# Moving statistics, short products and turns inside the key/value stage of a fused attention and GLU kernel

## The chip, the cores and the metric

The kernel runs on one core of a Trainium2 chip. The metric is the device time of one execution in microseconds. Five engines work beside each other, each through its own queue in order: TensorE (PE in the profile; its weight loads are PEld), VectorE (DVE), ScalarE (ACT), GpSimd (POOL) and SyncE (SP), which here issues DMA transfers. Engines wait for each other by semaphores.

## What is computed

One transformer block in float32 over 2048 rows x of 576 numbers: a layer norm, a linear attention of 32 heads of 18 numbers, and a gated branch that multiplies it.

```python
x = A_x
xn = _layernorm(x, axis=-1)
s = _A_ref(xn, A_wqkv, A_wo)
g = _silu(_B_ref(xn, B_w_gate, B_w_up, B_w_down))
return x + s * g
```

with, in the attention,

```python
phi = lambda t: jnp.where(t > 0, t + 1, jnp.exp(t)) + 1e-6
pq, pk = phi(q), phi(k)
kv = jnp.einsum("bhsd,bhse->bhde", pk, v)
z = jnp.einsum("bhsd->bhd", pk)
num = jnp.einsum("bhqd,bhde->bhqe", pq, kv)
den = jnp.einsum("bhqd,bhd->bhq", pq, z)[..., None] + 1e-6
o = num / den
return (lambda x, *d: x.transpose(*d))(o, 0, 2, 1, 3).reshape(B, S, D) @ wo
```

The branch B (gate, up, down with 4608 columns) takes most of the time and is not touched by the change.

## The kernel before

**Tiles and stages.** The rows are cut into 16 tiles of 128 (P). Four tiles are a block of 512 columns of the transposed x (TB = 4 blocks, TT = 4 tiles in each). The first 215 us or so are the attention, in stages: tiles 0 to 7 (keys and values), q of blocks 0 and 1, tiles 8 to 15 (N0 = 8), q of blocks 2 and 3, and the output products s. Then comes branch B. Every engine's instructions keep the order in which the program writes them (`keep_in_program_order`, line 120), so the order of the source is the order of each queue.

**A tile** (`kv_tile`, line 492). `x_mm(t, c)` multiplies x of tile t by the three parts c of the key and value weights, 14 products in each. `turn(t + 1)` and `place(t + 1)` prepare the next tile: from tile 4 on, TensorE turns the mean and the scale of each row into rows over all partitions (the tile `ms`, line 214: one product from `mv`, one from `st`), and `normalize` (line 228) subtracts and multiplies on VectorE (`x`, `xf_B`) and cuts the result into a high and a low word (`xo_B`, ScalarE and VectorE). `k_post` makes phi of the keys in two steps, c = 0 and c = 1: VectorE writes `e_k` and `pk`, ScalarE takes the exponential of `e_k` behind the second step, GpSimd adds both to the finished `pk`. `v_post` copies v into `va` on ScalarE, also in two steps (c = 1 and c = 2), and GpSimd fills `va`'s first column. `pk` and `va` take buffers from four slots, two tiles' worth. The list `mid_` runs between `place` and the second step of `k_post`; the list `end` between the third product group and the last `v_post`.

**Pairs.** In each even tile, behind the first product group, `kv_pair` adds the sums of the two tiles before to the bank `kv_a` (`kv_mm`, line 396): per tile ten products, two halves of five groups. Four groups have 72 columns, the fifth has 36. The halves go to two halves of the array's columns.

**Statistics.** `x_next(n)` (line 1427) does for an even n the statistics of tiles n and n + 1: four `BATCH_NORM_STATS2` (`bn`) and two aggregates (`mv`) on VectorE, a logarithm and an exponential on ScalarE (`st`), and four more small VectorE steps. From tile 4 on nothing else is left in it, so for odd n it does nothing. x itself comes in pairs of tiles by `load_x`, issued on SP behind tile 8 for tiles 12 and 13, and behind tile 10 for tiles 14 and 15.

**Forms of x.** `difference` and `form` make sums and differences of blocks (T1 to T4) for branch B. `form("T4")` at the end of tile 9 is one ScalarE copy (`xo_T`), VectorE's low words, and a store.

**q stages.** `q_store` and `q_hold` compute q of one block and group gi by 14 products; for gi = 4 (the columns of the fifth group, made together with k and v and kept in `qt`) there are four turns (line 526) instead. `phi` follows on ScalarE, VectorE and GpSimd. `q_store` also writes the result to memory by SP. The dictionaries `behind` (line 1492) and `ahead` (line 1521) list what runs behind each q step (block, group).

Of the kernel before, what the change touches and what calls it, by code (L numbers as in the profile page):

```python
# [31 lines left out]
WIDTHS = [GW, GW, GW, GW, D - 4 * GW]  # L32
# [59 lines left out]
def block_kernel(ctx, tc, x, xe, xt, wq_d, wkv_d, wo, wgu_d, wd_d, out):  # L92
# [9 lines left out]
    def own_bank(name):  # L102
        return ps.tile([P, 512], F32, tag="own", bufs=2, name=name)
# [18 lines left out]
    def act(*args, **kw):  # L122
        pin(nc.scalar.activation(*args, **kw))  # L123

    def vec(op, *args, **kw):
        pin(getattr(nc.vector, op)(*args, **kw))  # L126
# [42 lines left out]
    def spread(n0, n):  # L169

        bn = sb.tile([P, TT, 12], F32, tag="bn", bufs=2, name=f"bn_{n0}")
        mv = sb.tile([P, 2 * TT, 2], F32, tag="mv", bufs=4, name=f"mv_{n0}")
        for t in range(n):
            xs = xstat[(n0 + t) // 2][:, (n0 + t) % 2]
            for j in range(2):
                src = xs[:, j, 0:HALF] if n0 < TT else xs[:, j * HALF : (j + 1) * HALF]
                vec("bn_stats", out=bn[:, t, 6 * j : 6 * j + 6], in_=src)
            vec("bn_aggr", out=mv[:, t, :], in_=bn[:, t, :])
        st = sb.tile([P, 6, TT], F32, tag="st", bufs=4, name=f"st_{n0}")
        act(st[:, 0, 0:n], mv[:, 0:n, 1], AF.Ln, bias=eps_t)  # L180
        act(st[:, 2, 0:n], st[:, 0, 0:n], AF.Exp, scale=-0.5)
        vec("tensor_scalar", st[:, 1, 0:n], mv[:, 0:n, 1], LN_EPS, None, op0=ALU.add)
        mom[n0] = n, mv, st

    def scales(n0):

        n, mv, st = mom.pop(n0)
        v, r, c = (st[:, i, 0:n] for i in range(1, 4))
        if n == 1:
            vec("tensor_scalar", c, r, r, -0.5, op0=ALU.mult, op1=ALU.mult)  # L190
            vec("tensor_scalar", c, c, v, 1.5, op0=ALU.mult, op1=ALU.add)
            vec("tensor_scalar", c, c, r, None, op0=ALU.mult)
        else:
            vec("scalar_tensor_tensor", c, r, -0.5, r, op0=ALU.mult, op1=ALU.mult)
            vec("tensor_mul", c, c, v)
            vec("scalar_tensor_tensor", c, c, 1.5, r, op0=ALU.add, op1=ALU.mult)
        for t in range(n):
            scale_of[n0 + t] = mv[:, t, 0:1], c[:, t : t + 1]

    def center(n):  # L200

        if n >= TT:
            return
        xs = xstat[n // 2][:, n % 2]
        m, r = scale_of.pop(n)
        vec("tensor_scalar", xs, xs, m, r, op0=ALU.subtract, op1=ALU.mult)
# [85 lines left out]
    def difference(s, i):  # L292
        f = xf[s]
        nm, a, b, o = SUMS[i]
        vec("tensor_sub", f[o], f[a], f[b])
        f[nm] = f[o]
# [82 lines left out]
    acc = []  # L379
# [13 lines left out]
        act(e, e, AF.Exp, scale=-1.0)  # L393
        pool("tensor_add", o, o, e)

    def kv_mm(t):
        if t == 0:
            acc.append(own_bank("kv_a"))
        pk, va = pks.pop(t), vas.pop(t)
        for gi, wdt in enumerate(WIDTHS):  # L400
            for half in range(2):
                o, cs = kv_out(gi, half)
                mm(
                    o, va[:, 2 * gi + half, 0 : o.shape[0]],
                    pk[:, gi * GW + cs.start : gi * GW + cs.stop],
                    start=(t == 0 and gi == 0), stop=(t == S // P - 1),
                    skip_group_check=True,
                )
# [6 lines left out]
    pkv, pks, vas, es, qt = {}, {}, {}, {}, {}  # L415
# [76 lines left out]
    def kv_tile(t, mid_=(), end=()):  # L492

        ahead = t % (2 * TT) != 2 * TT - 1
        x_mm(t, 0)
        if t % 2 == 0:
            kv_pair(t)
        if ahead:
            turn(t + 1)
        k_post(t, 0)  # L500
        x_mm(t, 1)
        if ahead:
            place(t + 1)
            save(t + 1)
        run(list(mid_))
        k_post(t, 1)
        v_post(t, 1)
        x_mm(t, 2)
        run(list(end))
        v_post(t, 2)  # L510

    def kv_pair(t):

        for i in (t - 2, t - 1):
            if i in vas:
                kv_mm(i)

    ph, ph_d = {}, {}

# [20 lines left out]
    def q_store(tb, gi):  # L540
        if tb not in ph_d:
            ph_d[tb] = dr.tile([P, NHG, TBN], F32, name=f"phd_{tb}")
        o = gl_tile([P, TBN], f"ph_{tb}_{gi}")
        q_mm(tb, gi, o)
        dma(out=ph_d[tb][:, gi, :], in_=o)

    def q_hold(tb, i, gi):
        if tb not in ph:
            ph[tb] = big(i, [P, NHG, TBN], F32, f"ph_{tb}")
        q_mm(tb, gi, ph[tb][:, gi, :])  # L550
# [87 lines left out]
    def kv_wo(gi):  # L638

        if gi == 4:  # L640
            at["kvh"] = big(4, [P, 4, D], F32R, "kvh")
            at["kvl"] = big(5, [P, 4, D], F32R, "kvl")

            at["kv4"] = big(6, [P, 4, D], F32R, "kv4")
            pool("memset", at["kv4"][Q4:P, 1, :].bitcast(F32), 0.0)
        kvh, kvl, kv4 = at["kvh"], at["kvl"], at["kv4"]
        zc, mh = at["zc"], at["maskh"]
        wdt, k = (W4, P // 2 + W4 // 2 + 1) if gi == 4 else (GW, P)
        w = at["wo4"] if gi == 4 else at["wo"][:, gi]
        pw = []  # L650
        for c, cs in enumerate((slice(0, HALF), slice(HALF, D + 2))):
            pw.append(bank(f"kw_{gi}_{c}"))
            mm(
                pw[c][0:wdt, 0 : cs.stop - cs.start], at["kvm"][0:k, gi, 0:wdt], w[0:k, cs],
                start=True, stop=True,
            )
        r, x_ = slice(0, Q4 if gi == 4 else GW), slice(Q4, W4)
        z = pw[1][:, HALF : HALF + 1]

        def parts(hi, lo, rows):  # L660
            for c in range(2):
                cs = slice(c * HALF, (c + 1) * HALF)
                split(hi[:, cs], lo[:, cs], pw[c][rows, 0:HALF])

        if gi == 4:
            vec("tensor_copy", zx[x_], z[x_])
            parts(kv4[x_, 2, :], kv4[x_, 3, :], x_)
            for c in range(2):
                act(kv4[Q4:P, 0, c * HALF : (c + 1) * HALF], pw[c][r, 0:HALF], AF.Copy)

        vec(
            "tensor_scalar", zc[r, gi, :], mh[r, gi, :], z[r], None, op0=ALU.mult,
        )
        if gi == 4:
            parts(kv4[r, 0, :], kv4[r, 1, :], r)
        else:
            parts(kvh[r, gi, :], kvl[r, gi, :], r)
# [749 lines left out]
    def x_next(n):  # L1427

        if n % 2 == 0:
            spread(n, 2)  # L1430
            scales(n)
        center(n)
# [18 lines left out]
    for n in range(3, 2 * TT):  # L1451
        ends = []
# [20 lines left out]
    N0 = 2 * TT  # L1473

    def form(nm):
        keep(0, nm, build(0, nm, 12))

    def form_apart(nm):

        f = xf[0][nm]  # L1480
        store[0, nm] = d = dr.tile([P, 5, TBN], F32, name=f"kept_0_{nm}")
        hi, lo, last = (slot([P, 2, TBN], F32R, f"xo_0_{nm}_{i}") for i in range(3))
        act(hi, f[:, 0:2], AF.Copy)
        act(last[:, 0], f[:, 2], AF.Copy)
        vec("tensor_sub", lo, f[:, 0:2], hi.bitcast(F32))
        r = slice(KR, 2 * KR)
        vec("tensor_sub", last[r, 0], f[r, 2], last[r, 0].bitcast(F32))
        dma(out=d[:, 0:2], in_=hi.bitcast(F32))
        dma(out=d[:, 3:5], in_=lo.bitcast(F32))
        dma(out=d[:, 2], in_=last[:, 0].bitcast(F32))  # L1490

    behind = {
        (0, 0): [lambda: kv_pair(N0), lambda: spread(N0, 2), lambda: difference(0, 3)],
        (0, 1): [
            lambda: scales(N0), lambda: form("T1"), lambda: q_store(1, 4),
        ],
        (0, 2): [lambda: form_apart("T3")],
        (0, 3): [lambda: turn(N0)],
        (1, 0): [lambda: place(N0)],
# [5 lines left out]
            run(behind.get((tb, gi), []))  # L1505
    for n in range(N0, 2 * N0):
        ends = []
        if n < 2 * N0 - 2:
            ends.append(lambda n=n: center(n + 2) if n == N0 else x_next(n + 2))
        if n == N0 + 1:  # L1510
            ends.append(lambda: form("T4"))
        if n == 2 * N0 - 3:
            ends.append(load_wo)
        if n == 2 * N0 - 2:
            ends.append(make_sel)
        if n == 2 * N0 - 1:
            ends += [lambda i=i: difference(1, i) for i in range(3)]
        kv_tile(n, end=ends)
        if n in (N0, N0 + 2):
            load_x(n + 4, 2)  # L1520
    ahead = {
        (2, 0): [lambda: kv_pair(2 * N0), kv_done, spread_sel, lambda: difference(1, 3)],
        (2, 1): [lambda: kv_wo(4), lambda: q_hold(2, 7, 4)],
        (2, 2): [lambda: kv_wo(0), lambda: kv_wo(1), move_rows],
        (2, 3): [lambda: kv_wo(2), lambda: kv_wo(3)],
        (3, 0): [lambda: den(2), lambda: q_hold(3, 8, 4)],
# [117 lines left out]
```

## Time and profile before

| | |
|---|---|
| median of 3 runs | 1457.64 us (1456.2 to 1458.19) |
| the profiled execution | 1456.24 us |
| its span, first to last instruction | 1454.5 us |
| granted TensorE clock, mean | 1.000 |
| tiles 8 to 15 in the timeline | about 106.6 to 178.8 us |
| idle time of TensorE that the view of waits lists | 1.6 us at the start, 0.8 us in tile 11 |

In the timeline a row gives the start and duration in microseconds, the engine, the line (for recorded helpers that of the helper), the operation, output and inputs by the program's names, and in brackets the idle time of the engine before it with what ended it. Rows of several instructions are merged (x3). The chain of waits gives pieces that follow each other without overlap: start, duration, what. Matmuls overlap in the pipeline, so the duration of one is longer than the distance to the next. A float32 product is recorded as two matmuls.

### The profile page before, as it was taken

How to read it: one execution, taken by the hardware profiler on the slowest of the kernel's cores; microseconds unless marked ns; L12 is line 12 of the kernel's file. 1: busy time of each engine (PE TensorE's matmuls, PEld its weight loads, DVE VectorE, ACT ScalarE, POOL GpSimd, SP SyncE). 2: the span in 40 equal slices, each digit the busy share in tenths (PEclk: the TensorE clock that was granted, in tenths of full speed). 3: DMA queues.
4: the chain of work that ended last, by engine and by line, in shares of the span. 5: the costliest groups of instructions: out<-in, count | busy, mean ns of one | idle time of the engine just before them, and what ended most of it. 6: DMA issues, size and time to landing. Idle time of an engine off the chain costs nothing.

```text
span 1454.5 us, 22180 instructions
## 1 busy us (share of the span) xinstructions
PE 1447.7 (100%) x8286; PEld 1289.9 (89%) x8286; DVE 1149.5 (79%) x1605; ACT 561.3 (39%) x914; POOL 579.6 (40%) x520
## 2 busy tenths in 40 slices
PE   9999999999999999999999999999999999999998
PEld 8989989988888888888888888888889999999998
DVE  7787767376787887888777878778888978989888
ACT  6343355332222233322332232332235555545454
POOL 3342340235756567566475755667632000000000
PEclk9999999999999999999999999999999999999999
DMA  5543105521422315224242243323389887767886
GB/s 223 191 190 141 38 30 212 209 109 51 169 98 104 130 51 182 94 94 140 72 159 87 98 149 106 113 85 118 129 277 349 262 263 251 249 188 232 278 289 224
DMA packets 118085, 233.98 MB, mean 161 GB/s; under 512 B 11018, under 2 KB 44682, under 8 KB 116058
## 3 DMA queue, kind: packets, MB, share of 16 engines
q1 hardware_dynamic: 115178, 220.31, 45.0%
q0 software_dynamic: 2656, 12.06, 2.2%
q8 instruction: 65, 1.06, 0.3%
q14 instruction: 42, 0.34, 0.1%
q10 hardware_dynamic: 144, 0.20, 0.0%
HBM read 149.91 MB, written 82.58 MB: 160 GB/s over the span
## 4 chain that ended last, share of the span: by engine, by line
PE 98%; DVE 1%; ACT 0%; issue 0%; POOL 0%; DVEq 0%; ACTq 0%; POOLq 0%
PE bd L129 25%; PE al L859 16%; PE de L859 16%; PE ga L859 16%; PE kv L129 8%; PE be L859 8%; PE s L129 4%; PE q L129 4%; PE kv_a L129 1%; PE idle L129 0%; PE d L129 0%; PE kw L129 0%; PE b L129 0%; PE ms L214 0%; DVE acc L126 0%
## 5 line engine op out<-in xcount | busy, mean ns | idle before, releaser
L132 POOL TENSOR_TENSOR sm<-raw 128x384 f32<-128x384 f32 x72 | 75.2, 1044 | 145.9 <-DMA raw<-in_wgu_dram 120.6
L129 PE MATMUL kv<-wkv,xo_B 128*128 128x412 f32 (+2 forms) x662 | 125.7, 348 | 0.0
L129 PEld LDWEIGHTS kv<-wkv,xo_B 128*128 128x128 f32 x662 | 119.8, 188 | 1.4 <-DVE wkv L126 0.5
L126 DVE TENSOR_TENSOR wa<-sm,wa 128x768 fp32r<-128x768 f32 x72 | 92.3, 1282 | 36.1 <-ACT wa L123 35.2
L129 PE MATMUL bd<-w_head,hi 128*128 128x288 f32 x516 | 117.9, 294 | 0.0
L126 DVE TENSOR_TENSOR wb<-raw,wb 128x256 fp32r<-128x256 f32 (+1 forms) x108 | 102.1, 946 | 7.4 <-ACT wb L123 5.8
L126 DVE TENSOR_TENSOR wa<-raw,wa 128x256 fp32r<-128x256 f32 x72 | 66.3, 921 | 51.7 <-ACT wa L123 50.6
L123 ACT ACTIVATE hi<-raw_h 128x1024 fp32r<-128x1024 f32 x59 | 62.5, 1060 | 94.8 <-PE bd L129 64.8
L129 PE MATMUL bd<-w_end,hi 128*128 128x288 f32 x448 | 89.8, 294 | 0.0
L123 ACT ACTIVATE spot_h<-spot_h 128x512 f32<-128x512 f32 x49 | 30.7, 633 | 150.3 <-DVE spot_h L126 150.3
L129 PEld LDWEIGHTS bd<-w_head,hi 128*128 128x128 f32 x516 | 87.0, 188 | 0.1
L126 DVE TENSOR_TENSOR raw_h<-raw_h,hi 128x1024 fp32r<-128x1024 f32 x59 | 71.7, 1220 | 17.3 <-ACT hi L123 17.2
L129 PE MATMUL bd<-w_end,raw_h 128*128 128x288 f32 x264 | 77.9, 295 | 0.0
L123 ACT ACTIVATE wa<-sm 128x1152 fp32r<-128x1152 f32 x36 | 41.8, 1161 | 91.8 <-PE de L859 91.8
L123 ACT ACTIVATE u<-al 128x512 f32<-128x512 f32 x72 | 40.9, 593 | 89.5 <-PE al L859 56.3
L129 PEld LDWEIGHTS bd<-w_end,hi 128*128 128x128 f32 x448 | 71.9, 188 | 0.0
L129 PE MATMUL bd<-beside,raw_h 128*128 128x288 f32 x240 | 70.8, 295 | 0.0
L132 POOL TENSOR_TENSOR spot_h<-spot_h,spot_h 128x512 f32<-128x512 f32 x45 | 62.7, 1399 | 2.9 <-DVE spot_h L126 2.4
L859 PE MATMUL al<-xo_B,wa 128*128 128x512 f32 x252 | 63.0, 389 | 0.0
L859 PE MATMUL al<-xr_B,wa 128*128 128x512 f32 x252 | 63.0, 389 | 0.0
L859 PE MATMUL be<-xo_T,wa 128*128 128x512 f32 x252 | 63.0, 389 | 0.0
L859 PE MATMUL be<-xr_T,wa 128*128 128x512 f32 x252 | 63.0, 389 | 0.0
(274 smaller groups left out, 4039.9 us busy)
## 6 DMA issues: line engine op xcount, KB each, us to landing
raw_h<-hs SPq DMA_DIRECT2D x176, 256.0 KB
raw<-in_wgu_dram SPq DMA_DIRECT2D x36, 768.0 KB
hs<-spot_h SPq DMA_DIRECT2D x90, 256.0 KB
hs<-spot_g SPq DMA_DIRECT2D x80, 256.0 KB
b<-in_wd_dram SPq DMA_DIRECT2D x42, 432.0 KB
hs<-spot_m SPq DMA_DIRECT2D x38, 256.0 KB
raw_g<-hs SPq DMA_DIRECT2D x22, 256.0 KB
raw_a<-hs SPq DMA_DIRECT2D x20, 256.0 KB
```

The lines of the kernel that those rows point to most:

```text
L123: pin(nc.scalar.activation(*args, **kw))
L126: pin(getattr(nc.vector, op)(*args, **kw))
L129: pin(nc.tensor.matmul(*args, **kw))
L132: pin(getattr(nc.gpsimd, op)(*args, **kw))
L859: nc.tensor.matmul(o, w[0:rows, wi, :], xop[0:rows, xi, :], start=(start and n == 0), stop=(n == len(PASSES) - 1), skip_group_check=True,)
```

## The change

The statistics of tiles 12 and 13 run in the middle of tile 9 (so far at the end of tile 10), those of tiles 14 and 15 at the end of tile 11 (so far at the end of tile 12). In a pair, both tiles' products of four groups go first, then both tiles' products of the fifth group. The turns of q's columns for blocks 1 and 2 follow directly behind the pair's sums, where so far they came one q step later.

```diff
-    def kv_mm(t):
-        if t == 0:
+    def kv_mm(t, groups):
+        if not acc:
             acc.append(own_bank("kv_a"))
-        pk, va = pks.pop(t), vas.pop(t)
-        for gi, wdt in enumerate(WIDTHS):
+        pk, va = pks[t], vas[t]
+        for gi in groups:
...
     def kv_pair(t):
 
-        for i in (t - 2, t - 1):
-            if i in vas:
-                kv_mm(i)
+        pair = [i for i in (t - 2, t - 1) if i in vas]
+        for groups in (range(4), (4,)):
+            for i in pair:
+                kv_mm(i, groups)
+        for i in pair:
+            del pks[i], vas[i]
...
     behind = {
-        (0, 0): [lambda: kv_pair(N0), lambda: spread(N0, 2), lambda: difference(0, 3)],
-        (0, 1): [
-            lambda: scales(N0), lambda: form("T1"), lambda: q_store(1, 4),
+        (0, 0): [
+            lambda: kv_pair(N0), lambda: q_store(1, 4), lambda: spread(N0, 2),
+            lambda: difference(0, 3),
         ],
+        (0, 1): [lambda: scales(N0), lambda: form("T1")],
...
     for n in range(N0, 2 * N0):
         ends = []
-        if n < 2 * N0 - 2:
-            ends.append(lambda n=n: center(n + 2) if n == N0 else x_next(n + 2))
+        middle = [lambda: x_next(N0 + 4)] if n == N0 + 1 else []
+        if n == N0 + 3:
+            ends.append(lambda: x_next(N0 + 6))
         if n == N0 + 1:
             ends.append(lambda: form("T4"))
...
-        kv_tile(n, end=ends)
+        kv_tile(n, middle, ends)
...
     ahead = {
-        (2, 0): [lambda: kv_pair(2 * N0), kv_done, spread_sel, lambda: difference(1, 3)],
-        (2, 1): [lambda: kv_wo(4), lambda: q_hold(2, 7, 4)],
+        (2, 0): [
+            lambda: kv_pair(2 * N0), kv_done, lambda: q_hold(2, 7, 4), spread_sel,
+            lambda: difference(1, 3),
+        ],
+        (2, 1): [lambda: kv_wo(4)],
```

## The prediction

> **What bounds the kernel now.** I read the page first: busy time by engine, and the chain that ended last.
>
> ```profile
> PE 1447.7 (100%) x8286; PEld 1289.9 (89%) x8286; DVE 1149.5 (79%) x1605; ACT 561.3 (39%) x914; POOL 579.6 (40%) x520
> PE 98%; DVE 1%; ACT 0%; issue 0%; POOL 0%; DVEq 0%; ACTq 0%; POOLq 0%
> ```
>
> TensorE is occupied for the whole span, so only two things count: TensorE time taken away, and TensorE stalls removed or made. The view of who waited for whom, for TensorE alone, has one stall behind the start:
>
> ```profile
> PE ms L214 <- DVE st L126: 0.8, 1, 0.8
> ```
>
> The timeline around it (start, duration, engine, operation) shows how it comes about, in the stage of tiles 8 to 15:
>
> ```profile
> 132.35 0.82 DVE L126 BATCH_NORM_STATS2 bn<-x 128x6 f32<-128x288 f32 x2
> 134.13 0.21 DVE L126 BATCH_NORM_AGGREGATE mv<-bn 128x2 f32<-128x12 f32 x1
> 134.52 0.27 PE L214 MATMUL ms<-ident,mv 128*128 128x128 f32 x1
> 134.94 0.16 DVE L126 SCALAR_TENSOR_TENSOR st<-st 128x2 f32<-128x2 f32 x1 [0.39 <-ACT st L123]
> 135.33 0.16 DVE L126 SCALAR_TENSOR_TENSOR st<-st 128x2 f32<-128x2 f32 x1
> 135.41 0.58 DVE L126 TENSOR_SCALAR e_k<-kv 128x416 f32<-128x416 f32 x1
> 135.54 0.32 PE L214 MATMUL ms<-ident,st 128*128 128x128 f32 x1 [0.76 <-DVE st L126]
> ```
>
> Statistics of tiles 12 and 13 begin on VectorE at 132.35, the end of tile 10. They end at 135.33 + 0.16 = 135.49, and TensorE, which turns tile 12's mean and scale in tile 11, starts 0.05 us later. VectorE goes on to e_k at 135.41: a block of statistics occupies it for 135.41 - 132.35 = **3.06 us**, a wait for ScalarE's logarithm and exponential included.
>
> **Term 1, the stall removed.** The chain in order of time gives its full price, against the same turn in tile 13:
>
> ```profile
> 135.87 7.71 PE kv L129 x42
> ...
> 152.95 0.22 PE ms L214 x2
> 153.17 7.75 PE kv L129 x42
> ```
>
> The two turns of tile 13 take 0.22 us on the chain. In tile 11 the first begins at 134.52, some 0.16 before its chain time (a 0.27 us record that ends 0.11 after the next starts), so 134.68; products follow at 135.87, which is 1.19 us against 0.22. With the statistics a tile earlier this **saves 0.97 us** (0.76 if only the stall in brackets goes).
>
> **Term 2, a stall made.** The same 3.06 us of VectorE now stand in the middle of tile 9, after tile 10 is placed and ahead of tile 9's second k step. The timeline of that place:
>
> ```profile
> 122.23 0.33 DVE L126 TENSOR_SCALAR e_k<-kv 128x160 f32<-128x160 f32 x1
> 123.42 1.45 POOL L132 TENSOR_TENSOR pk<-pk,e_k 128x576 f32<-128x576 f32 x1 [4.91 <-ACT e_k L123]
> 124.80 0.12 POOL L132 MEMSET va<- 128x10 f32 x1
> 124.88 0.49 ACT L123 ACTIVATE va<-kv 128x252 f32<-128x252 f32 x2
> 125.01 1.92 DVE L126 TENSOR_TENSOR xo_T<-xf_B,xo_T 128x1024 fp32r<-128x1024 f32 x2 [2.23 <-ACT xo_T L123]
> 125.23 1.38 PE L129 MATMUL kv_a<-pk,va 128*64 128x72 f32 x40
> ```
>
> At 122.23 VectorE makes e_k of tile 9; ScalarE's exponential, then the sum on GpSimd that completes pk of tile 9 (to 124.87), and the fill of va's first column (to 124.92) follow it in a row. At 125.23 TensorE begins the sums of tiles 8 and 9, which read pk and va. They are ready by a margin of only 0.31 us for the pair, and about 1 us for tile 9, whose products come after tile 8's. VectorE works in order, so the inserted block moves this whole row by 3.06 us: pk and va's column of tile 9 are complete at 124.92 + 3.06 = 127.98, and with the 0.05 us seen above TensorE starts on tile 9 at 128.03. It would be ready for tile 9 at:
>
> ```profile
> 143.57 1.31 PE kv_a L129 x40
> ```
>
> 40 records for 20 products, 0.066 us a product; the changed order puts eight of tile 8 first, 125.23 + 8 x 0.066 = 125.76. **New stall: 128.03 - 125.76 = 2.27 us.** Lower bound: the block without VectorE's 0.39 us of waiting for ScalarE (the row at 134.94), 2.67 us, so 1.88. Upper bound: all of va must be there, also ScalarE's last copies behind the fourth form's copy, 124.88 + 0.49 + 3.06 = 128.43, so 2.72. I take 2.27, since va is written in parts and the first four products of tile 9 read the earlier ones; the later parts come while these run.
>
> Nothing can hide this: TensorE's queue is in order, and behind the sums wait the turn of tile 11 and all further products. What is late next is VectorE's fourth form (125.01 to 128.07), then k of tile 10, then x of tile 11, all by 3.06 us, while TensorE is late by 2.27 - a difference of 0.8. Tile 11's operand stands at:
>
> ```profile
> 106.78 2.63 PE kv L129 x14
> ...
> 129.66 0.54 ACT xo_B L123
> ```
>
> Tile 11's first products ran from about 134.52 - 2.63 = 131.89, ScalarE's first half was there at 130.20: 1.7 us of margin, of which 0.8 goes. No second stall. From 131.8 on VectorE is relieved of the 3.06 us that stood in tile 10, and catches up.
>
> **Term 3, tile 14's statistics** move from tile 12's end to tile 11's. No stall goes with them. They land in idle VectorE time:
>
> ```profile
> 143.61 0.59 DVE L126 TENSOR_SCALAR e_k<-kv 128x416 f32<-128x416 f32 x1 [2.98 <-PE kv L129]
> 144.41 0.59 DVE L126 TENSOR_SCALAR pk<-kv 128x416 f32<-128x416 f32 x1 [0.21 <-PE kv_a L129]
> ```
>
> 3.06 us into 2.98: e_k of tile 12 is 0.08 late, then waits for TensorE again. ScalarE's logarithm and exponential now stand ahead of va of tile 11, which the pair at 143.5 reads; VectorE comes free at 143.61 - 2.98 = 140.63, the means are there 1.99 later (134.13 + 0.21 - 132.35), the two ScalarE steps take until VectorE's next step, 0.6 (134.94 - 134.34), the copy 0.49: 143.7, against the fifth product of tile 11 at 143.5 + 12 x 0.066 = 144.3. **Cost 0**; without that cover up to 0.5.
>
> **Term 4, short products last.** In a pair the two products of 36 columns of the first tile stand between those of 72. Four looks into the pair at 125.23, each row starting with the oldest record still running:
>
> ```profile
> 125.81 0.41 PE L129 MATMUL kv_a<-pk,va 128*37 128x36 f32 x7
> ...
> 125.84 0.39 PE L129 MATMUL kv_a<-pk,va 128*64 128x72 f32 x6
> ...
> 125.94 0.42 PE L129 MATMUL kv_a<-pk,va 128*64 128x72 f32 x8
> ...
> 126.00 0.42 PE L129 MATMUL kv_a<-pk,va 128*64 128x72 f32 x8
> ```
>
> Long records follow each other by 0.06, a short one takes 0.03, but the first long one behind a short keeps the array 0.10 to 0.09 before the next: 0.03 lost, because its weights load under a short product. With all short ones last that happens once less in a pair. Eight pairs: **0.24 us saved** (0 if shorts in a row cost as much, 0.32 at 0.04). The first tile's pk and va come free by eight products, 0.5 us, later; behind this waits pk of the next even tile (the 144.41 row), and behind it x of the tile after, which has the margin of a whole third product group, 2.63 us. No cost.
>
> **Term 5, turns of q's columns right behind the sums.** Chain pieces:
>
> ```profile
> 79.08 3.20 PE q L129 x14
> 82.28 1.31 PE kv_a L129 x40
> 83.59 3.42 PE q L129 x14
> 87.02 0.44 PE q L526 x4
> ...
> 189.88 3.23 PE q L129 x14
> ...
> 199.50 0.59 PE q L526 x4
> ```
>
> q's products cost 3.20, but 3.42 behind the sums: 0.22 for leaving their split array. The four turns cost 0.44, and 0.59 where they follow other split products (at 199.50): 0.15. So turns take over the break for 0.07 less, twice; in the second stage q's products then follow kw's directly, 3.23 against 3.20, 0.03 given back. **0.11 us saved** (0 to 0.4). The Trainium skill ("TensorEngine Tiling (Array Packing)", Key Properties) says that changing the tiling mode drains TensorE, whatever comes next; by that alone this term would be 0 and the sum 0.11 higher. The rows differ by what follows, so I go by them.
>
> Each moved turn brings its phi: two ScalarE steps, one of VectorE, one of GpSimd, and in the first stage a store on SP's queue. There they stand ahead of tile 8's statistics, which are turned three q steps of 3.2 us later, and SP's store goes out ahead of the stores of the form T1 instead of behind them. In the second stage they go ahead of the spread of the selection on ScalarE and GpSimd, which is read first behind the turns at 199.50, and stay behind the masked sums that kw reads a q step later. TensorE's q steps of 3.2 us cover them: cost 0.
>
> **Sum:** -0.97 + 2.27 + 0 - 0.24 - 0.11 = **+0.95 us**, bounds -0.97 + 1.88 - 0.32 - 0.4 = +0.2 and -0.76 + 2.72 + 0.5 = +2.5. The profiled execution took 1456.24 (span 1454.5), the low end of the three runs; the median is 1457.64. So 1457.2 for an execution like the profiled one and **1458.6** for a median.
>
> **Rivals.**
>
> *No stall at the pair (the change gains).* If pk of tile 9 is completed in time, because the statistics fit into idle VectorE time, terms 1, 4 and 5 are left: -1.32, or 1456.3. For it: VectorE waits 2.23 us for ScalarE at 125.01. Against it: that idle time lies behind tile 9's e_k, and the block goes ahead of it. Chance 0.19.
>
> *The stall slows TensorE's clock (slower than before).* The start shows what a cold array costs:
>
> ```profile
> 1.59 5.39 PE idle L129 x24
> ...
> 187.93 1.95 PE kw L129 x8
> ...
> 134.00:136.00 2.00, 1.24 (x8) 0.92 (x7) 1.47 (x8) 1.06 (x5) 0.50 (x2) 1.00 0.84 340
> ```
>
> 24 records of 128 columns took 0.225 each; kw's of 288 columns, hot, 0.244, which is 0.108 for 128. That is 24 x 0.117 = 2.8 us lost in one warm-up. If 2.27 us without products are enough, the change ends at 0.95 + 2.8 = +3.75, 1461.4. Against it: the stall of 134.5 left the granted clock at 1.00. It decides once the stall is long enough to trip the clock. The Trainium skill ("TensorE: Matmul & The Clock Gate", Part 1) puts that at an idle window of about 3.4 us; by that rule 2.27 us doesn't trip it, while no run yet shows a stall between 1 and 3.4. Chance 0.05.
>
> *Tile 12's x isn't there at 122.23.* It was read at 132.35 so far; now any lateness of its load is added to the new stall one to one, and over 2 us late the change is slower by more than can be told from none.
>
> ```profile
> 114.69 0.46 SPq L135 DMA_DIRECT2D x<-in_xt_dram  x1
> ...
> 120.00:122.00 2.00, 2.00 (x13) 2.00 (x13) 1.78 (x6) 0.99 (x2) 0.00 (x0) 1.00 0.03 11
> ```
>
> Its second part is issued at 114.69, and from 120 the DMA engines stand still (busy share 0.03, 11 GB/s), so it had landed. At 1 us late: 1459.6. Chance 0.06.
>
> **How the numbers follow.** The forecast has 0.70, with its own range 1457.8 to 1460.1. Two parts in a thousand, 2.9 us, are about what this kernel's measurement tells from no change. The forecast and the gaining rival both lie within that. Slower by more: the clock (0.05), half of the late load (0.03), a tail of the forecast: 0.09. Faster by more has no mechanism in these rows, as TensorE has only 1 us of stalls to give: 0.03. Same: 0.88. The range goes from the gaining rival less 0.7 for the scatter of runs, 1455.6, to 1461.0, short of the clock rival.
>
> **What would show it.** Right: TensorE's waits list a new one of some 2.3 us (1.9 to 2.7) before sums kv_a, released by GpSimd's pk or va, near 126 us, and no longer ms behind st; VectorE's e_k of tile 9 stands near 125.3; q after a pair shows 3.20 again and turns 0.59. Wrong: no such wait (then a gain of 1.3), a wait at tile 11's or 12's products besides, or a clock under 1.00 after 128.

## The result and the profile after

| | before | changed |
|---|---|---|
| median, 16 runs each | 1456.71 us (1456.2 to 1459.12) | 1459.51 us (1457.79 to 1461.79) |
| ratio | | 1.0018, 95% interval [1.001, 1.0025] |
| span of the profiled execution | 1454.5 us | 1456.9 us |

The change costs about 2.6 us (1456.71 x 0.0018), between 1.5 and 3.6 by the interval. The forecast was +0.95 us and 1458.6.

TensorE's waits after the change, waited for and releaser, us in total, times, longest:

```profile
PE kv_a L129 <- POOL va L132: 2.0, 1, 2.0
PE idle L129 <- POOL ident masks.py:199: 1.6, 1, 1.6
PE xt L222 <- PE idle L129: 0.3, 1, 0.3
PE kv L129 <- ACT xf_B L123: 0.2, 1, 0.2
```

The wait of the turn of tile 12 is gone. A longer one stands before the sums of a pair. The last two rows belong to the start, which took longer in this execution: at tile 8 everything is late by 0.80 us against the trace of before (its first products begin at 107.58 on the chain, before at 106.78). The start varies by itself: in the later profiles of the experiments tile 8 begins at 107.43 in the kernel before and at 106.94 in the changed one.

The timeline of tile 9 and its pair after the change:

```profile
123.04 0.82 DVE L126 BATCH_NORM_STATS2 bn<-x 128x6 f32<-128x288 f32 x2
...
126.03 0.72 PE L129 MATMUL kv_a<-pk,va 128*64 128x72 f32 x16
126.09 0.32 DVE L126 TENSOR_SCALAR e_k<-kv 128x160 f32<-128x160 f32 x1
...
127.27 1.40 POOL L132 TENSOR_TENSOR pk<-pk,e_k 128x576 f32<-128x576 f32 x1 [8.01 <-ACT e_k L123]
...
128.61 0.11 POOL L132 MEMSET va<- 128x10 f32 x1
...
128.78 0.99 PE L129 MATMUL kv_a<-pk,va 128*64 128x72 f32 x24 [2.02 <-POOL va L132]
...
137.71 0.27 PE L214 MATMUL ms<-ident,mv 128*128 128x128 f32 x1
```

The block of statistics takes VectorE from 123.04 to 126.09, 3.05 us; e_k, pk and va of tile 9 follow it. TensorE does eight products of tile 8 and stands until va's first column is there at 128.72. Less the 0.80 of the start, the products of tile 9 begin at 127.98; predicted were 128.03.

The chain, in order of time:

```profile
83.24 1.29 PE kv_a L129 x40
84.53 0.59 PE q L529 x4
85.12 9.54 PE q L129 x42
...
107.58 2.63 PE kv L129 x14
...
128.78 0.99 PE kv_a L129 x24
...
137.87 0.22 PE ms L214 x2
138.09 7.75 PE kv L129 x42
...
200.42 1.23 PE d L129 x40
```

The turns of q's columns follow the pair for 0.59, then three q steps cost 9.54, which is 3.18 each. The two turns of tile 12 take 0.22, as in other tiles. And in the trace of before the same first products of the sums d stood here:

```profile
198.27 1.23 PE d L129 x40
```

From tile 8's first products to them it was 198.27 - 106.78 = 91.49 us, and is 200.42 - 107.58 = 92.84: **+1.35 us** from tile 8 to these sums, in a trace whose clock does not fall there. In the two later profiles the same way takes 91.54 and 92.79 us, +1.25. The median moved by about twice that. So the experiments had two questions: is the stall all that the edits cost, and where is the rest?

### The profile page after: what moved, and what is told of

It is laid out like the page before. It is cut to its first block, busy times and chain, and to the rows that moved or that the text cites. A ratio compares the mean times of both kernels' runs of the same rounds, so it can differ in the third digit from the quotient of the medians.

```text
span 1456.9 us, 22178 instructions
## 1 busy us (share of the span) xinstructions
PE 1448.3 (99%) x8286; PEld 1289.5 (89%) x8286; DVE 1152.1 (79%) x1605; ACT 561.4 (39%) x914; POOL 580.1 (40%) x520
## 4 chain that ended last, share of the span: by engine, by line
PE 97%; DVE 1%; ACT 0%; DMA 0%; issue 0%; POOL 0%; SPq 0%; DVEq 0%; ACTq 0%
PE bd L129 25%; PE ga L862 16%; PE al L862 16%; PE de L862 16%; PE kv L129 8%; PE be L862 8%; PE s L129 4%; PE q L129 4%; PE kv_a L129 1%; DMA rw<-in_wkv_dram 0%; PE d L129 0%; PE kw L129 0%; PE b L129 0%; PE ms L214 0%; DVE acc L126 0%
## 5 line engine op out<-in xcount | busy, mean ns | idle before, releaser
L862 PE MATMUL ga<-xo_B,wb 128*128 128x512 f32 x252 | 63.1, 389 | 0.0
L862 PE MATMUL ga<-xr_B,wb 128*128 128x512 f32 x252 | 63.0, 389 | 0.0
```

What stands on the lines that cost most here:

```text
L862: nc.tensor.matmul(o, w[0:rows, wi, :], xop[0:rows, xi, :], start=(start and n == 0), stop=(n == len(PASSES) - 1), skip_group_check=True,)
```

## The experiments

**Both kernels again, and the two halves of the change.** The first two kernels are unchanged; of every execution the mean granted TensorE clock is compared with its time. The third has only this:

```diff
+        middle = [lambda: x_next(N0 + 4)] if n == N0 + 1 else []
+        if n == N0 + 3:
+            ends.append(lambda: x_next(N0 + 6))
...
+        kv_tile(n, middle, ends)
```

The fourth has everything but this.

> The kernel before, unchanged. Theory (the new stall itself, plus a fall of TensorE's clock that the stall sets off in some executions): all executions show a granted clock of 1.000 and the median stays near 1456.7 us. Rival (the extra time beyond the stall is scatter of the start, where the first weights landed 0.85 us later in the profiled execution of the changed kernel): clocks under 1.000 turn up here as often as in the changed kernel, where 10 of 16 executions showed 0.998 or 0.999.

> The changed kernel, unchanged. Theory: about 1459.5 us, ratio 1.002, a granted clock of 0.998 or 0.999 in more than half of the executions, and those executions slower by 1 to 2 us than the ones at 1.000. Rival: time and clock do not go together.

> Only the statistics are moved; products of a pair and turns stay as before. Theory: a wait of 1.9 to 2.0 us before the second tile's sums near 126 us, no wait before the turn of tile 12; from the traces +1.1 to +1.4 us, and with executions at a lower clock a median of +2.5 to +3, that is 1459 to 1460 us, ratio 1.002. Rival (the extra comes from the other edits or from the start): +1.1 to +1.4, ratio 1.001, clocks at 1.000.

> The changed kernel with the statistics back where they were: only the order of a pair's products and the place of the turns differ from before. Theory: no new wait, the 0.8 us wait of the turn of tile 12 is there again, clocks 1.000, and the predicted saving of 0.24 + 0.11 = 0.35 us, about 1456.4 us. Rival: the extra time stays, 1457.5 us or more.

| kernel | median | ratio to before | executions at clock 0.998 |
|---|---|---|---|
| before again | 1457.17 us | 1.0002 [0.9993, 1.0011] | 0 of 11 |
| changed again | 1459.02 us | 1.0014 [1.0004, 1.0023] | 2 of 11 |
| statistics alone | 1459.03 us | 1.0015 [1.0007, 1.0024] | 2 of 11 |
| all but the statistics | 1457.82 us | 1.0005 [0.9996, 1.0013] | 0 of 11 |

The statistics alone bring the whole loss: from tile 8 to the first sums d their trace takes 92.83 us, that of all but the statistics 91.49, as before. The other edits neither gain nor lose what these runs can tell (the expected 0.35 us is under that). Their median, 1457.82 us, lies on the side of the rival that the extra time stays, and not near the expected 1456.4; but the interval holds 1, its list of TensorE's waits has no new one in these stages, and the profiled execution, which is the one of 1457.82 us, lists a wait of 0.6 us in branch B, which no edit touches. A clock of 0.998 came in the two kernels with the stall and in none without it; the changed kernel's first 16 runs had it 4 times more, and of the 33 runs of before beside these none. One expectation failed: 0.999 came in before as well (12 of those 33, no slower than the rest), so it says nothing. The profiles show one source of it: in the one of before that has 0.999 the clock is 1.00 up to 1454 us and 0.56 from there to the end at 1455.9, behind the last product, where TensorE has nothing left to do. In the changed kernel's first 16 runs the six at 1.000 averaged 1458.8 us, the four at 0.998 1460.3; in the second set it was 1458.5 for five and 1459.6 for two, with one at 1.000 as slow as 1460.2. That fits a clock that falls in some executions, but none of the profiles so far showed it fall at the stall.

**A longer stall.** The statistics in the middle are done twice, with the same values:

```diff
-            for j in range(2):
+            for j in list(range(2)) * reps:
...
-        middle = [lambda: x_next(N0 + 4)] if n == N0 + 1 else []
+        middle = [lambda: spread(N0 + 4, 2, 2), lambda: scales(N0 + 4)] if n == N0 + 1 else []
```

> The changed kernel with each of the four BATCH_NORM_STATS2 in the middle of tile 9 done twice (the same values written again), so that VectorE's block is 1.6 us longer (0.82 + 0.77 of the rows of one block). Theory (the stall follows VectorE's block one to one, and the longer TensorE stands still, the more executions lose clock): a wait of 2.02 + 1.6 = 3.6 us before the pair's second tile, clocks of 0.998 or less in most executions, and a time more than 1.6 us above the changed kernel, about 1462 us. Rival (no part of the clock): the wait grows alike, executions as before at 1.000 or 0.999, and the time grows by 1.6 us, 1460.6. Second rival (something else than pk and va of tile 9 releases the pair): the wait stays near 2.0 us.

1461.33 us, ratio 1.003 [1.0019, 1.0042]. The wait grew to 3.5 us:

```profile
129.37 1.48 PE L129 MATMUL kv_a<-pk,va 128*64 128x72 f32 x24 [3.47 <-POOL va L132]
```

Its profile caught the clock; busy time by stretch (PE, PEld, DVE, ACT, POOL, then the granted clock, DMA share, GB/s):

```profile
128.40:128.80 0.40, 0.00 (x0) 0.00 (x0) 0.00 (x0) 0.40 (x1) 0.40 (x1) 0.58 0.00 0
128.80:135.20 6.40, 5.83 (x38) 5.64 (x39) 5.49 (x9) 2.17 (x6) 0.52 (x2) 0.50 0.48 205
135.20:135.60 0.40, 0.40 (x4) 0.40 (x3) 0.37 (x2) 0.00 (x0) 0.00 (x0) 0.89 0.02 0
```

The clock falls to half within the stall and stays there for 6.8 us (0.58 in 0.40 us puts the fall at 128.46, 0.89 the rise at 135.29). Four of six executions showed 0.998, two 0.999; for these two a fall at the stall isn't shown.

**The changed kernel again, for its profile, and a stall between.** Two more executions of the changed kernel as it is, and a kernel in which only one of the two instructions is repeated (`for j in (0, 1, 1)[0 : 1 + reps]`).

> The changed kernel once more, for its profile. Theory (a stall of 2.0 us costs TensorE its clock in a part of the executions): if this execution is one of those at 0.998, the profile shows a stretch at half clock that begins within some us of the stall near 126 us and costs 1 to 2 us on top of it; if it is one at 1.000, no such stretch. Rival: an execution at 0.998 or 0.999 loses its clock somewhere else, or at the start alone.

> As the look before: a stretch at half clock behind the stall if the execution is slow, none if it is not; a stretch anywhere else speaks for the rival.

> The changed kernel with one of the two BATCH_NORM_STATS2 of each tile in the middle of tile 9 done twice: a block 0.8 us longer, a stall of 2.8 us between the 2.0 of the changed kernel and the 3.5 that lost its clock in every execution. Theory (the longer the stall, the more executions lose the clock): clocks of 0.998 or 0.999 in more executions than with 2.0 us and in fewer than all, a median of 1460 to 1461 us. Rival (a sharp threshold between 2.0 and 3.5 us): all executions or none.

The first execution, 1460.71 us, has what was missing. Its TensorE timeline and its stretches:

```profile
125.14 0.72 PE L129 MATMUL kv_a<-pk,va 128*64 128x72 f32 x16
127.89 1.40 PE L129 MATMUL kv_a<-pk,va 128*64 128x72 f32 x24 [2.02 <-POOL va L132]
...
138.19 0.27 PE L214 MATMUL ms<-ident,mv 128*128 128x128 f32 x1
```

```profile
127.60:128.00 0.40, 0.11 (x2) 0.11 (x4) 0.03 (x1) 0.40 (x2) 0.23 (x2) 1.00 0.00 0
128.00:128.40 0.40, 0.40 (x10) 0.40 (x12) 0.40 (x1) 0.40 (x3) 0.00 (x0) 0.52 0.00 0
128.40:131.20 2.80, 2.80 (x27) 2.68 (x24) 2.72 (x5) 0.10 (x1) 0.00 (x0) 0.50 0.19 80
...
131.40:131.60 0.20, 0.20 (x2) 0.19 (x2) 0.20 (x1) 0.00 (x0) 0.00 (x0) 0.92 0.84 358
```

Right behind the 2.02 us stall, from 128.02 to 131.43 (by the shares of 0.52 and 0.92), TensorE runs at half clock, 3.4 us. The 24 records of the pair take 1.40 us instead of 0.99, and from their start to the turn of tile 12 it is 138.19 - 127.89 = 10.30 us, where in the first profile it is 137.71 - 128.78 = 8.93: **1.4 us lost on top of the stall.** The second execution, 1458.32 us, has the same stall without any such stretch:

```profile
125.38 0.72 PE L129 MATMUL kv_a<-pk,va 128*64 128x72 f32 x16
128.12 0.98 PE L129 MATMUL kv_a<-pk,va 128*64 128x72 f32 x24 [2.02 <-POOL va L132]
```

Both show a mean clock of 0.999: in the second it falls only behind the last product (0.86 from 1450 us to the end). The first is 2.4 us slower, and the clock is not all of it: its waits also list 1.2 us in branch B (`ga` behind VectorE's `u`), which the second doesn't have and which come and go in other executions too.

The stall between became 3.0 us long, where 2.8 was expected:

```profile
128.98 1.47 PE L129 MATMUL kv_a<-pk,va 128*64 128x72 f32 x24 [3.01 <-POOL va L132]
```

It gave 1460.61 us, ratio 1.0026 [1.0016, 1.0036], with six of nine executions at 0.998 or 0.997, and in its profile a stretch at half clock too (0.50 from 128.6 to 131.8 us). So there is no sharp length between 2.0 and 3.5 us at which it starts: 6 of 27 timed executions of the changed kernel were at 0.998 with 2.0 us, 6 of 9 at 0.998 or less with 3.0, 4 of 6 with 3.5. More executions lose the clock at 3.0 than at 2.0; whether the share still grows up to 3.5 these few can't tell.

**Hiding the statistics.** VectorE's part goes between ScalarE's copy and VectorE's low words of T4; ScalarE's part and what follows (`spread_end`, `scales`) go behind tile 9's last copy of va; `False` leaves ScalarE's part out of `spread`.

```diff
+    def form_around(nm, work):
...
+        act(o[:, 0:3], f, AF.Copy)
+        work()
+        vec("tensor_sub", o[:, 3:5], f[:, 0:2], o[:, 0:2].bitcast(F32))
...
-            ends.append(lambda: form("T4"))
+            ends.append(lambda: form_around("T4", lambda: spread(N0 + 4, 2, False)))
...
+        if n == N0 + 1:
+            spread_end(N0 + 4)
+            scales(N0 + 4)
```

The first kernel has this on top of the change, without the statistics in the middle; the second has it with the moved turns alone, on the kernel before; the third is the moved turns alone; the last repeats the second.

> The changed kernel with VectorE's statistics of tiles 12 and 13 put between ScalarE's copy and VectorE's low words of the form T4, where VectorE waits 2.2 us for ScalarE, and ScalarE's logarithm and exponential behind the last copy of va of tile 9. Theory: neither the wait before the pair (pk of tile 9 is no longer behind the block) nor the one of the turn of tile 12 remains; against before the trace is 0.95 us shorter by the turn of tile 12 and 0.1 us by the other edits, clocks at 1.000 as in before: about 1455.9 us, ratio 0.9993. Rival (the move of the statistics costs in itself, wherever they stand in tile 9): a wait before the pair or before tile 11's products of 1 us or more, 1457.5 us or above.

> The kernel before with those hidden statistics and the moved turns of q's columns, products of a pair in the old order and tile 14's statistics where they were. Theory: as the kernel with hidden statistics on top of the whole change, within 0.2 us, as short products last are worth under 0.1 us: about 1455.9 us. Rival (short products last are worth the predicted 0.24 us): 0.24 us slower than that kernel in the trace from the first pair to the output products.

> The kernel before with the moved turns of q's columns alone. Theory: in the trace the stretch from the last tile of a q stage's stage to its end is 0.07 to 0.12 us shorter in each of the two stages, all pairs as before. Rival: no difference, if leaving the split array costs the same whatever follows (the rule of the Trainium skill, TensorEngine Tiling (Array Packing), Key Properties).

> The kernel with hidden statistics and moved turns again, to tell it from before: ratio 0.9992 within 0.0003, with the executions of the run before an interval that lies under 1. Rival: no difference from before, ratio 1.000.

| kernel | median | ratio to before |
|---|---|---|
| changed, statistics hidden | 1455.88 us | 0.9994 [0.9985, 1.0003] |
| before, statistics hidden, turns moved | 1455.83 us | 0.9991 [0.9982, 1.0000] |
| the same again | 1455.49 us | 0.9990 [0.9981, 0.9998] |
| before, turns moved (one run) | 1456.58 us | - |

The first kernel's timeline in tile 9:

```profile
122.89 0.82 DVE L126 BATCH_NORM_STATS2 bn<-x 128x6 f32<-128x288 f32 x2
...
123.57 1.48 ACT L123 ACTIVATE xo_T<-xf_B 128x1536 fp32r<-128x1536 f32 x1
...
125.08 1.92 DVE L126 TENSOR_TENSOR xo_T<-xf_B,xo_T 128x1024 fp32r<-128x1024 f32 x2 [0.20 <-ACT xo_T L123]
...
125.30 1.36 PE L129 MATMUL kv_a<-pk,va 128*64 128x72 f32 x40
...
125.48 0.31 ACT L123 ACTIVATE st<-mv,eps_t 128x2 f32<-128x2 f32 x1
```

VectorE's wait for ScalarE's copy shrinks from 2.23 to 0.20 us, with the statistics in it, and the pair runs without a stall, as does the turn of tile 12. None of the 33 executions of these kernels showed a clock under 0.999. The version with the old order of products is no slower than the one with the new. Its second measurement, 1.4 us under before, is the only one whose interval lies wholly under 1. The traces show the gain too: from the pair of tile 6 to the first sums d it takes 132.56 us in both its profiles, in the kernel before 133.64.

The chains price the two small edits. A pair with short products last, in the kernel with all but the statistics:

```profile
64.96 1.38 PE kv_a L129 x40
...
82.67 1.29 PE kv_a L129 x40
```

Against 1.31 in the old order a pair saves 0.02, but the pair of tile 6 costs 1.38: its second tile's products come two products sooner and meet GpSimd's end of pk and va:

```profile
64.89 1.45 PE L129 MATMUL kv_a<-pk,va 128*64 128x72 f32 x40
...
65.31 0.12 POOL L132 MEMSET va<- 128x10 f32 x1
```

va's column is there at 65.43, where in this order the first product of tile 5 was due at 64.89 + 8 x 0.065 = 65.41. The eight pairs themselves save some 0.07 us together (7 x 0.02 - 0.07). But the x products behind a pair take longer in the new order; here those of tile 12, first in the chain after the change, then in the chain before:

```profile
147.49 7.75 PE kv L129 x42
```

```profile
145.25 7.70 PE kv L129 x42
```

The two kernels with hidden statistics differ in the order of the pairs, and in tile 14's statistics, which neither waits for. From the pair of tile 6 to the first sums d the new order takes 132.61 us and the old one 132.56, so nothing of the saving is left there. The turns, in the kernel that moves nothing else:

```profile
82.17 1.31 PE kv_a L129 x40
83.48 0.59 PE q L526 x4
84.07 9.57 PE q L129 x42
...
162.02 0.36 PE ms L214 x2
...
198.01 1.23 PE d L129 x40
```

1.31 + 0.59 + 9.57 = 11.47, against 1.31 + 3.42 + 0.44 + 6.40 = 11.57 before: 0.10 saved in the first stage. In the second it is 198.01 - 162.02 = 35.99 us from tile 15's turns to the first sums d, before 198.27 - 162.23 = 36.04: 0.05 saved.

## Why the prediction was right, and where it was not

The mechanism and the sign were right, and the time lies in the range. That the median came as near as 0.9 us is partly luck: the forecast set out from 1457.64 us, the median of three runs, where 16 gave 1456.71, and it added 0.95 where the change costs about 2.6. The two errors point opposite ways and partly cancel.

**Term 1, the stall removed:** right. Tile 12's turns take 0.22 on the chain, 0.97 less than before by the same count.

**Term 2, the stall made:** right in place, releaser and size. VectorE's block of 3.05 us delays pk and va's column of tile 9 one to one, TensorE starts on that tile within 0.05 us of the time named. The view of waits lists 2.02 of the 2.27 us, because TensorE's last record before it ends at 126.03 + 0.72 = 126.75; counted as in the prediction, from 126.03 + 8 x 0.066 = 126.56, it is 2.22. Terms 1 and 2 together are +1.30, and the statistics alone cost 92.83 - 91.49 = 1.34. Undoing this move alone took the loss out of the trace, hiding it turned it into a gain.

**Term 3:** right; tile 14's statistics cost nothing, and the pair of tile 12 has no wait.

**Term 4, short products last:** the step that failed. 0.24 us was forecast; the pairs' own pieces give about 0.07, and the way from the pair of tile 6 to the first sums d shows no saving at all (132.61 against 132.56 us). A pair does get shorter, by 0.02 where 0.03 was forecast (1.31 to 1.29), but in tile 6 the earlier products of the second tile wait, and the products behind a pair, which the forecast took as unchanged, take up to 0.05 longer (7.70 to 7.75). That the order makes the second tile's products due earlier was used in term 2, and not asked of the other pairs. The cause that the prediction names for the break, weights that load under a short product, was not tested.

**Term 5, the turns:** right, 0.15 for 0.11. The rows decided here between a price of leaving the split array that is the same whatever comes next (no saving) and one that depends on it: the moved turns cost 0.59 behind the pair, 0.15 more than the 0.44 elsewhere, and q's products behind them no extra in the first stage and 0.03 in the second, while right behind the pair it was 0.22.

The sum of the terms is +0.95. On the chain from the pair of tile 6 to the first sums d, which holds all but two pairs, the change costs 134.90 - 133.64 = +1.26 us, and +1.17 in the two later profiles. Terms 1, 2 and 5 as measured make +1.2 of that. So the difference to the forecast, 0.2 to 0.3, is in the main term 4's; what is left is too small to assign.

**The clock rival** got 0.05, and it holds in a part of the executions. The forecast took it for all or nothing, with 2.8 us, a whole warm-up; it costs 1.4 us where a stretch of 3.4 us at half clock follows the stall, and nothing elsewhere. The rows of the start from which the 2.8 us came carry a granted clock of 1.00, so no trace here shows that a low clock made them slow. The evidence against it, that the stall of 134.5 left the clock at 1.00, was 0.8 us of stall and said nothing of 2. The sign that the prediction names, a clock under 1.00 after 128, is absent in the first profile and there in the execution of 1460.71 us.

How many executions have such a stretch can be bounded. 3.4 us at half clock take 0.0012 off the mean of an execution, so one at 1.000 has none. One at 0.998 very likely has one, since no execution without the stall came under 0.999. At 0.999 it stays open. That makes 4 to 10 of the first 16 executions, and 2 to 6 of the second 11. Those at 1.000 give the price of the stall without the clock: 1458.77 us on average against 1457.05 before in the first set, 1458.46 against 1456.90 in the second, so +1.7 and +1.6, where the chain has +1.2 to +1.3; with six and five executions the difference is within their scatter. All executions of the changed kernel average 1459.62 and 1458.88 us, so the clock adds about 0.8 and 0.4 us to the average.

**The other rivals:** no stall at the pair: wrong, as argued; VectorE's idle time lies behind e_k, and only putting the statistics there made that rival true. Tile 12's x late: wrong, the block began as soon as VectorE was free.

## What to carry to other kernels

Where TensorE is the bound and other engines work in order, moving a block of work earlier on one of them moves everything behind it: look up who waits for the next instruction of that queue, and put the block into an idle time of its own engine rather than ahead of it. A stall of TensorE can cost more than its length: here 2 us were enough, though not in every execution, so a single profile can miss that part. Compare the clock of many executions, and look in the trace where it falls, as a fall behind the last product costs nothing. A reordering that removes a break makes something due earlier; ask each place where it runs, not one.

## What the runs showed of the hardware

A wait of 2.0 us was enough for TensorE's clock to fall to half for 3.4 us, in some executions of one kernel and not in others; 3.0 and 3.5 us did it more often, the last for 6.8 us in the profiled execution. A stall of 0.8 us left the clock at 1.00. The Trainium skill ("TensorE: Matmul & The Clock Gate", Part 1) names an idle window of about 3.4 us, that runs freely of the kernel's start. The stretches agree with the window's length (3.4, and twice that), and that the same stall trips it or not agrees with a window that isn't tied to the program. But the stall doesn't have to fill the window: 2.0 us did. That it depends on how the stall lies in the window was not tried.

The ends of the traces show as well that length alone doesn't decide. Behind the last product TensorE stands idle for some 4.2 us in every profile. In the first profile of before with hidden statistics and moved turns (last product to 1449.65) the clock is 1.00 up to 1451.8 us and 0.50 from 1452.0, so it falls after 2.2 us; in the trace of before it is 1.00 for the first 3.6 us and 0.58 in the last 0.6; with the moved turns alone it stays at 1.00 through all 4.3 us. No trace shows it fall anywhere else than there and at the stall.
